# Talking-heads attention and a squared-ReLU FFN on one core: larger reserves in the planner, its order searched anew, and the reciprocals of the row sums on another engine

## The chip, the cores and the metric

The kernel runs on one core of a Trainium2 chip, as one launch. The time is device microseconds of one execution. Matrix products run on TensorE (PE), evictions from PSUM and elementwise work on ScalarE (ACT) and VectorE (DVE), small elementwise work and the loads' DMA issues on GpSimd (POOL), other DMA issues on SyncE (SP). Each engine works through its own list of instructions in order; semaphores tie the lists together.

## The reference

Eight batches, twelve heads, 448 positions, head dimension 64. The attention mixes the heads twice: the scores before the softmax with `w_pre`, the probabilities after it with `w_post`. An FFN with squared ReLU follows, 768 to 2048 to 768.

```python
scores = scale * np.matmul(q, k.transpose(0, 1, 3, 2))      # (8, 12, 448, 448)
scores = np.einsum('bhij,hg->bgij', scores, w_pre)
scores = scores - np.max(scores, axis=-1, keepdims=True)
attn = np.exp(scores)
attn = attn / (np.sum(attn, axis=-1, keepdims=True) + 1e-09)
attn = np.einsum('bhij,hg->bgij', attn, w_post)
attn_out = np.matmul(attn, v)
x = attn_out.transpose(0, 2, 1, 3).reshape(8 * 448, 768)
h = np.maximum(x @ w_in, 0.0)                               # (3584, 2048)
out = h * h @ w_out                                         # (3584, 768)
```

## The kernel before, in words

The kernel is written as some thousands of tasks. A task is a few instructions on one engine, with the tasks that it depends on, a planned cost and a priority. A planner (`_Plan`) plays the whole kernel through on the host when the program is built, and the program then has each engine's tasks in the planned order, with a semaphore wait wherever a dependency crosses engines. Nothing is decided at run time but how long each wait lasts; a wait stands only at the start of a task.

The stages for each batch, with the lines of their matmuls:

- **T** (L832, L836): q and k are transposed on PE into `qkt`.
- **QK** (L974, L981, L988): scores of one tile of 128 (or 64) query rows, evicted by DVE or ACT (L524, L523) into `stage`, one of two slots. In the first batch a direct form (**spr**, L915) gives part of the scores in the layout wanted.
- **Relayout** (`emit_rel`, L1033 and L1035): SP issues DMAs from `stage` to `dring`. They bring the twelve heads of ten query rows onto the partitions, a chunk of 120 rows. `dring` has 16 slots.
- **pre** (L1059, L1066, L1074): two chunks at a time are multiplied with the spread `w_pre`; ACT takes the exp (L1099) into `pring` (10 slots) and gives the row sums.
- **rec and fold** (L1122 and L1124, L1132): the reciprocal of the row sums is taken for a pair of chunks, `rinv`, and multiplied into a copy of the spread `w_post`, `wk2s`. For the first ten chunks both run on DVE, after that on POOL: there the reciprocal is a power of -1.
- **post** (L1164): `pring` times `wk2s` gives the mixed and normalized probabilities, transposed, evicted into `a2t`.
- **AV** (L1221, L1242) into `xt`; **F1** (L1293, L1301) with relu on ACT or DVE (L1338, L1339) and the square on DVE (L1348) into `h2t`; **F2** (L1432, L1440, L1380 for the last two tiles) into `osb`, one of two slots, and an output DMA issued by SP (L1478).

PE's units stand in ten queues (T, QK, pre, post, AV, spr, two of F1, two of F2). `ORDER` is a string with one character for each unit: which queue is next, and in which shape of the array it runs where a unit has more than one (rows, whole array, or quadrants). `next_unit` follows it, and TensorE never departs from it. All other engines take, among the tasks that are ready in the plan, the one that can start first; tasks marked FLEX (the evictions) go to ACT or DVE, wherever they are planned to end first. The string was found by a search that is not part of the kernel, against the planner's constants.

Those constants are estimates of the chip. `MODE_SWITCH` is charged where PE's shape changes. PE's instructions come in blocks of `BLOCK` = 256; `fetch` gives the planned time from the crossing of one block's end until the next block is there:

```python
return FETCH[0] + FETCH[1] * part["load"] + FETCH[2] * part["move"]
```

`part` is how much is moving in the two classes of DMAs, and `fetch_wait` puts the missing time before a unit. DMAs are of kind "load" (q, k, v, weights, and the outputs of the last two tiles) or "move" (the relayouts, and the other outputs). A DMA's data count as there at the end of its transfer plus `DMA_END` of its kind:

```python
t.end = max(t.end, now + DMA_END[t.dma[0]])
```

The DVE cost of a reciprocal is planned as 82 ns of the queue and 160 ns to the result, that on POOL as 700 and 750.

Of the kernel before, what the change touches and what calls it, by code (L numbers as in the profile page):

```python
# [7 lines left out]
ALU = mybir.AluOpType  # L8
DT = mybir.dt
# [4 lines left out]
DVE = "dve"  # L14
POOL = "pool"
# [4 lines left out]
MODE_SWITCH = 100.0  # L20
ACT_BIAS = 14.5
BLOCK = 256
FETCH = (2700.0, 2300.0, 1500.0)
EVENTS = {"tr": 0.12, "qk": 0.72, "di": 0.2, "sp": 0.3, "po": 0.61, "pr": 1.1, "av": 0.43, "o0": 0.43}
DMA_START = {"move": 2590.0, "load": 2640.0, "big": 1680.0}
DMA_AHEAD = 1600.0
DMA_END = {"move": 1450.0, "load": 1300.0}
INF = float("inf")
CODES = "0123456789abcdefghijklmnopqrst"
ORDER = (  # L30
    "00005bb05b0555555555555555555c12c555555513223555552c5001c353c00153355255233355555b332c22"
    "44443002h1g1b2q1h332g2236gh313c6722133hh31233gh6131hb2424443b32g26gh7q2b7371c63q1711r736"
    "2qh32002932t121j33933282b2s3c83338004224441200bgh11181c3s311s133s322rghg22b72b6h3163q633"
    "q32r42244413rbbh2ggb2002h716371623763q223837c738c33i3832bgh112rg0204244b20041328111ic31i"
    "3c3i33911tc11t22bj3c393c39342414431j313j2bqb2b62731762236733h3200q2162r21h13633g32r22728"
    "02000s131i113i14242b4334222931t333t111922813i3138422443411i332q2b6b2r2brb2gq0023733r3633"
    "qbrbq2rg2r200bh22913j12009111j3c381c383c3s313sc342442224193139111t333t2422444228318131i3"
    "13s32q2bqr227b3h2b2g733q333q20b6r120h2q0262000h7119331t111j33ct2228383138131ib4242224418"
    "3138331i24244413832q2bq2r2bh236331q33hgb21g72000r102h2173633633h24244420ttb2092b9238111i"
    "133i333i2t22btb2btbb2t238338331i42244431s31q2262713r1161733qh32qb2g2r2b273733r33gg12s22i"  # L40
    "22ss42244483i33s33i2qr262h2933933t33jq4q444hgqg6rgqhrh7ihgh6hgrhgg7hrqjjsjjit8isitijj"
)


# [72 lines left out]
class _Plan:  # L117
# [86 lines left out]
    def dma_next(self, go=False):  # L204
# [26 lines left out]
        if go:  # L231
# [5 lines left out]
            self.moving[t.dma[0]].pop(0)  # L237
            t.end = max(t.end, now + DMA_END[t.dma[0]])
            self._finish(t)
# [10 lines left out]
    def fetch(self, at):  # L250
        part = {}
        for q, xs in self.moving.items():
            part[q] = min(1.0, sum(x[1] for x in xs if x[0] <= at + 500.0) / 2500.0)
        return FETCH[0] + FETCH[1] * part["load"] + FETCH[2] * part["move"]

# [116 lines left out]
def bass_talking_heads_attention__then__ffn_squared_relu_kernel(  # L372
# [42 lines left out]
    with ExitStack() as es:  # L415
        def sb(name, shape, dtype):
            return es.enter_context(nc.sbuf_tensor(name, list(shape), dtype))
# [26 lines left out]
        rowsum = sb("rowsum", [128, B * NCP, 1], DT.float32)  # L444
# [2 lines left out]
        goods = sb("goods", [1, 128], DT.float32)  # L447
        flag = sb("flag", [1, 1], DT.int32)
        rinv = sb("rinv", [128, NPS, 1], DT.float32)
        minus1 = sb("minus1", [128, 2, 1], DT.float32)  # L450
        sb("align", [128, 64], DT.uint8)
        w_in_sb = sb("w_in_sb", [128, NFT, FF], DT.bfloat16)
        w_out_sb = sb("w_out_sb", [128, NFFT, F], DT.bfloat16)
# [38 lines left out]
        def program(guard):  # L492
# [9 lines left out]
            def add(name, engine, fn, deps, cost, prio, mode=None, group=None, instrs=0):  # L502
                return plan.add(name, engine, fn, deps, cost, prio, "ctr", 1, mode, group=group,
                                instrs=instrs)
# [28 lines left out]
            def fn_init(eng, en):  # L533
                eng.memset(mask[:, :, :], 1.0)
                eng.memset(wk1[:, :], 0.0)
                eng.memset(wrep[:, :], 0.0)
                eng.memset(wrepf[:, :], 0.0)
                eng.memset(maskf[:, :], 0.0)
                eng.memset(wkf[:, :, :], 0.0)
                eng.memset(wk2b[:, :, :], 0.0)  # L540
                eng.memset(rowsum[:, NCP - 1::NCP, :], 1.0)
                eng.memset(minus1[:, :, :], -1.0)
                return eng.memset(ident[:, :], 0.0)

            t_init = add("init", DVE, fn_init, [], {DVE: (950.0, 1050.0)}, -3e6)

            def fn_init2(eng, en):
# [127 lines left out]
            def members(g0):  # L675
                return (g0, g0 + 1) if g0 % NCP + 1 < NCH else (g0,)

            pairs = [b * NCP + c for b in range(B) for c in range(0, NCH, 2)]
            pre_of, exp_of, fold_of, post_of, a2_of = {}, {}, {}, {}, {}
# [366 lines left out]
            def old_users(g):  # L1046
                x = g - g % 2 - NPS
                return [d.get(y) for d in (post_of, fold_of) for y in (x, x + 1)]

            def emit_pre(g0):  # L1050
# [37 lines left out]
                for x, g in enumerate(gs):  # L1088
                    after_pre(g, t_pre, gr, x)

            def after_pre(g, t_pre, gr, x):
                b, c = divmod(g, NCP)
                pr = g % NPS

                def fn_exp(eng, en):
                    if guard:
                        return eng.activation(pring[:, pr, 0:S], ps[:, gr.banks[x], 0:S], AF.Exp,
                                              bias=nmax[:, pr, :], accum_out=rowsum[:, g, :])
                    return eng.activation(pring[:, pr, 0:S], ps[:, gr.banks[x], 0:S], AF.Exp,  # L1099
                                          accum_out=rowsum[:, g, :])  # L1100

                def fn_max(eng, en):
                    return eng.tensor_reduce(nmax[:, pr, :], ps[:, gr.banks[x], 0:S], AX.X, ALU.max,
                                             negate=True)

                t_max = None
                if guard:
                    t_max = add("max%d_%d" % (b, c), DVE, fn_max, [t_pre] + old_users(g),
                                {DVE: (540.0, 630.0)}, b * 1000.0 - 900 + c)
                t_exp = add("exp%d_%d" % (b, c), ACT, fn_exp, [t_pre, t_init, t_max] + old_users(g),  # L1110
                            {ACT: (517.0, 650.0)}, b * 1000.0 - 900 + c)
                exp_of[g] = t_exp
                gr.readers[x].append(t_exp)
                g0 = g - g % 2
                if g != members(g0)[-1]:
                    return
                n = g - g0 + 1
                p0 = g0 % NPS

                def fn_rec(eng, en):  # L1120
                    if en == POOL:
                        return eng.tensor_tensor(rinv[:, p0:p0 + n, :], rowsum[:, g0:g0 + n, :],  # L1122
                                                 minus1[:, 0:n, :], ALU.pow)
                    return eng.reciprocal(rinv[:, p0:p0 + n, :], rowsum[:, g0:g0 + n, :])  # L1124

                t_rec = add("rec%d_%d" % (b, c), DVE if g < 10 else POOL, fn_rec,
                            [exp_of[g0], t_exp] + old_users(g),
                            {DVE: (82.0, 160.0), POOL: (700.0, 750.0)}, b * 1000.0 - 900 + c)

                def fn_fold(eng, en):  # L1130
                    i0 = wk2b[:, :, :].rearrange("p a b -> p (a b)").unsqueeze(1)
                    return eng.tensor_tensor(  # L1132
                        wk2s[:, p0:p0 + n, :], i0.to_broadcast([128, n, PR]),
                        rinv[:, p0:p0 + n, :].to_broadcast([128, n, PR]), ALU.mult)

                t_fold = add("fold%d_%d" % (b, c), DVE if g < 10 else POOL, fn_fold,
                             [t_rec, t_wk2] + old_users(g),
                             {POOL: (330.0, 370.0), DVE: (200.0, 280.0)},
                             b * 1000.0 - 900 + c)
                t_fold.two = True  # L1140
                for y in members(g0):
                    fold_of[y] = t_fold
# [555 lines left out]
```

## Time and profile before

| | |
|---|---|
| three runs | 534.83, 539.58 and 539.79 us, median 539.58 us |
| the profiled execution | 537.8 us, span of its instructions 536.0 us |
| mean granted TensorE clock | 0.988 |
| busy: PE, ACT, DVE, POOL | 508.0, 412.3, 379.9, 290.8 us |
| POOL's reciprocals (L1122) | 179, 702 ns mean, 125.2 us |
| DVE's reciprocals (L1124) | 5, 155 ns mean |

The profile is one execution. Busy times are of the engine's own instructions. A row such as "PE ps L1074 <- DMA dring<-stage: 3.4, 4, 1.6" says that PE, before instructions of line 1074 that write `ps`, stood idle for 3.4 us in all, 4 times, at most 1.6 us, and that a DMA from `stage` to `dring` ended it. "issue" stands where no semaphore ended the wait. A wait for several things is put down to the one that came last by the profile. The rows of a timeline give start, duration, engine, line, operation, what it writes and reads, how many were merged, and in brackets the idle time before.

### The profile page before, as it was taken

How to read it: one execution, taken by the hardware profiler on the slowest of the kernel's cores; microseconds unless marked ns; L12 is line 12 of the kernel's file. 1: busy time of each engine (PE TensorE's matmuls, PEld its weight loads, DVE VectorE, ACT ScalarE, POOL GpSimd, SP SyncE). 2: the span in 40 equal slices, each digit the busy share in tenths (PEclk: the TensorE clock that was granted, in tenths of full speed). 3: DMA queues.
4: the chain of work that ended last, by engine and by line, in shares of the span. 5: the costliest groups of instructions: out<-in, count | busy, mean ns of one | idle time of the engine just before them, and what ended most of it. 6: DMA issues, size and time to landing. Idle time of an engine off the chain costs nothing.

```text
span 536.0 us, 24801 instructions
## 1 busy us (share of the span) xinstructions
PE 508.0 (95%) x10441; PEld 332.8 (62%) x10441; DVE 379.9 (71%) x806; ACT 412.3 (77%) x1181; POOL 290.8 (54%) x524
## 2 busy tenths in 40 slices
PE   8979999999999889989999899999989999989996
PEld 4435676667776546656566565666547766657963
DVE  7868977797987678765878768876857868536510
ACT  5979998888977878887787798888857888955421
POOL 9837788427954667446843587336844345522000
PEclk9989999999999999999999999999989999998999
DMA  9998999547964689457973689447963467532013
GB/s 172 192 184 145 196 183 193 112 87 146 178 154 75 137 183 173 93 127 135 180 166 67 140 150 224 92 91 163 193 134 64 105 141 142 113 72 61 3 29 93
DMA packets 81997, 70.87 MB, mean 132 GB/s; under 512 B 14038, under 2 KB 78422, under 8 KB 81878
## 3 DMA queue, kind: packets, MB, share of 16 engines
q1 hardware_dynamic: 48326, 46.40, 35.8%
q0 software_dynamic: 33392, 22.59, 31.0%
q8 instruction: 86, 1.41, 1.1%
q14 instruction: 33, 0.27, 0.1%
q10 hardware_dynamic: 160, 0.20, 0.1%
HBM read 45.63 MB, written 11.01 MB: 106 GB/s over the span
## 4 chain that ended last, share of the span: by engine, by line
PE 76%; DMA 7%; ACT 5%; DVE 4%; SPq 3%; issue 3%; POOL 0%; DVEq 0%; POOLq 0%
PE ps L1440 20%; PE ps L1301 17%; PE ps L1293 9%; PE ps L1164 6%; PE ps L1074 6%; DMA dring<-stage 5%; PE ps L1242 5%; SPq L1033 3%; ACT pring L1099 3%; PE ps L988 3%; PE ps L1380 2%; PE ps L1432 2%; PE ps L915 2%; DVE stage L524 2%; PE ps L836 2%
## 5 line engine op out<-in xcount | busy, mean ns | idle before, releaser
L1122 POOL TENSOR_TENSOR rinv<-rowsum,minus 128x2 f32<-128x2 f32 (+1 forms) x179 | 125.2, 702 | 185.9 <-ACT pring L1099 185.1
L1099 ACT ACTIVATE pring<-ps 128x448 bf16<-128x448 f32 x360 | 192.6, 563 | 23.0 <-PE ps L1074 13.2
L524 DVE CAST a2t<-ps 128x480 bf16<-128x480 f32 (+1 forms) x209 | 126.6, 641 | 37.6 <-PE ps L1164 36.7
L1440 PE MATMUL ps<-w_out_sb,h2t 64*128 64x384 bf16 (+1 forms) x1728 | 141.7, 324 | 0.2
L524 DVE CAST stage<-ps 128x448 bf16<-128x448 f32 x168 | 99.9, 618 | 31.1 <-PE ps L981 11.4
L1301 PE MATMUL ps<-xt,w_in_sb 64*64 64x448 bf16 (+4 forms) x1728 | 109.5, 329 | 0.1
L1440 PEld LDWEIGHTS ps<-w_out_sb,h2t 64*128 64x128 bf16 (+1 forms) x1728 | 75.3, 97 | 43.3 <-issue 2.0
L523 ACT ACTIVATE a2t<-ps 128x480 bf16<-128x480 f32 (+1 forms) x159 | 85.9, 580 | 20.8 <-PE ps L1164 20.0
L523 ACT ACTIVATE stage<-ps 128x448 bf16<-128x448 f32 x138 | 72.2, 556 | 18.7 <-PE ps L988 6.5
L1099 ACT ACTIVATION_READ_ACCUMULATOR pring<-ps 128x1 f32 x360 | 81.8, 227 | 0.0
L1301 PEld LDWEIGHTS ps<-xt,w_in_sb 64*64 64x64 bf16 (+1 forms) x1728 | 60.4, 103 | 29.8 <-issue 2.3
L1164 PEld LDWEIGHTS ps<-wk2s,pring 60*128 60x128 bf16 x2880 | 57.4, 94 | 28.0 <-issue 7.1
L1132 POOL TENSOR_TENSOR wk2s<-wk2b,rinv 128x120 bf16<-128x120 bf16 (+1 forms) x179 | 69.0, 388 | 10.2
L1164 PE MATMUL ps<-wk2s,pring 60*128 60x60 bf16 x2880 | 64.8, 187 | 4.4 <-issue 2.6
L1348 DVE TENSOR_TENSOR h2t<-h1t 128x448 bf16<-128x448 bf16 (+2 forms) x176 | 54.7, 336 | 11.2 <-ACT h1t L1338 10.1
L1074 PE MATMUL ps<-dring,wk 64*64 64x448 bf16 (+1 forms) x592 | 53.0, 360 | 10.0 <-DMA dring<-stage 3.4
L1293 PE MATMUL ps<-xt,w_in_sb 128*128 128x220 bf16 (+2 forms) x480 | 59.1, 276 | 0.0
L1338 ACT ACTIVATE h1t<-ps 128x448 bf16<-128x448 f32 (+2 forms) x88 | 39.1, 450 | 20.4 <-PE ps L1293 11.2
L1339 DVE TENSOR_SCALAR h1t<-ps 128x448 bf16<-128x448 f32 (+2 forms) x88 | 42.7, 492 | 16.5 <-PE ps L1301 13.1
L1293 PEld LDWEIGHTS ps<-xt,w_in_sb 128*128 128x128 bf16 x480 | 43.8, 98 | 12.3 <-issue 2.8
L523 ACT ACTIVATE osb<-ps 128x384 f32<-128x384 f32 x31 | 15.1, 492 | 27.2 <-PE ps L1432 8.6
L1242 PE MATMUL ps<-a2t,vraw 128*64 128x228 bf16 (+1 forms) x640 | 35.2, 261 | 0.0
(78 smaller groups left out, 464.5 us busy)
## 6 DMA issues: line engine op xcount, KB each, us to landing
dring<-stage SPq DMA_DIRECT2D x264, 105.0 KB
out_dram<-osb SPq DMA_DIRECT2D x45, 192.0 KB, 3.5
qraw<-in_q_dram POOLq DMA_DIRECT2D x42, 112.0 KB, 5.1
kraw<-in_k_dram POOLq DMA_DIRECT2D x42, 112.0 KB, 5.1
dring<-stage SPq DMA_DIRECT2D x70, 52.5 KB
w_in_sb<-in_moe_w_in_dram POOLq DMA_DIRECT2D x8, 384.0 KB, 10.0
w_out_sb<-in_moe_w_out_dram POOLq DMA_DIRECT2D x8, 384.0 KB, 8.8
vraw<-in_v_dram POOLq DMA_DIRECT2D x21, 128.0 KB
```

Source lines behind the costliest of these rows:

```text
L523: return eng.activation(o, i_, AF.Copy)
L524: return eng.tensor_copy(o, i_)
L1074: r_ = eng.matmul(ps[64 * y:64 * y + 64, gr.banks[x], 0:S], wk1[64 * x:64 * x + 64 - R0 * x, 64:128], dring[64 * x:64 * x + 64 - R0 * x, ( ...
L1099: return eng.activation(pring[:, pr, 0:S], ps[:, gr.banks[x], 0:S], AF.Exp, accum_out=rowsum[:, g, :])
L1122: return eng.tensor_tensor(rinv[:, p0:p0 + n, :], rowsum[:, g0:g0 + n, :], minus1[:, 0:n, :], ALU.pow)
L1132: return eng.tensor_tensor(wk2s[:, p0:p0 + n, :], i0.to_broadcast([128, n, PR]), rinv[:, p0:p0 + n, :].to_broadcast([128, n, PR]), ALU.mult)
L1164: r_ = eng.matmul(ps[:, gr.banks[x], o0:o0 + PR], pring[64 * x:64 * x + PR, pr + y, j0:j0 + 2 * PJ], wk2s[64 * x:64 * x + PR, pr + y, :], ...
L1242: r_ = eng.matmul(ps[kk * 64:kk * 64 + 64, g.banks[x_], x * n:(x + 1) * n], vraw[:, h, s, :], a2t[half][:, s, h, a0:a0 + n], start=(rest a ...
L1293: r_ = eng.matmul(ps[:, g.banks[ph], 0:n], w_in_sb[:, ft, t * 128:(t + 1) * 128], xt[:, ft, c0:c1], start=(ft == 0), stop=(ft == NFT - 1))
L1301: r_ = eng.matmul(ps[z:z + w, g.banks[x], 0:n], w_in_sb[64 * y:64 * y + 64, ft, t * 128 + z:t * 128 + z + w], xt[64 * y:64 * y + 64, ft, c ...
L1348: return eng.tensor_tensor(h2t[:, t16, o0:o0 + n], h1t[:, s, 0:n], h1t[:, s, 0:n], ALU.mult)
L1440: r_ = eng.matmul(ps[z:z + w, g.banks[hh], 0:FH], h2t[64 * y:64 * y + 64, t16, col + z:col + z + w], w_out_sb[64 * y:64 * y + 64, t16, hh ...
```

## The change

Three things: two of the planner's constants, the order string, and the engine of the reciprocals.

```diff
-FETCH = (2700.0, 2300.0, 1500.0)
+FETCH = (3500.0, 2300.0, 1500.0)
...
-DMA_END = {"move": 1450.0, "load": 1300.0}
+DMA_END = {"move": 2000.0, "load": 1300.0}
...
 ORDER = (
-    "00005bb05b0555555555555555555c12c555555513223555552c5001c353c00153355255233355555b332c22"
...
-    "22ss42244483i33s33i2qr262h2933933t33jq4q444hgqg6rgqhrh7ihgh6hgrhgg7hrqjjsjjit8isitijj"
+    "0000b15555011505555555555555552c5555555051325530cc51555cc3c233003555c352315553155533ccc2"
...
+    "s228i244438333i22283s3393t322t933rqr46444h7hghgghqghggghgiirqh7hgh8hr6gsjg8ttj88j98jj"
 )
...
-        minus1 = sb("minus1", [128, 2, 1], DT.float32)
...
-                eng.memset(minus1[:, :, :], -1.0)
...
                 def fn_rec(eng, en):
-                    if en == POOL:
-                        return eng.tensor_tensor(rinv[:, p0:p0 + n, :], rowsum[:, g0:g0 + n, :],
-                                                 minus1[:, 0:n, :], ALU.pow)
                     return eng.reciprocal(rinv[:, p0:p0 + n, :], rowsum[:, g0:g0 + n, :])
 
-                t_rec = add("rec%d_%d" % (b, c), DVE if g < 10 else POOL, fn_rec,
-                            [exp_of[g0], t_exp] + old_users(g),
-                            {DVE: (82.0, 160.0), POOL: (700.0, 750.0)}, b * 1000.0 - 900 + c)
+                t_rec = add("rec%d_%d" % (b, c), DVE, fn_rec, [exp_of[g0], t_exp] + old_users(g),
+                            {DVE: (82.0, 160.0)}, b * 1000.0 - 900 + c)
```

The whole string of 965 characters is replaced. The fold keeps its engine. Since the other engines' orders and the choice of ACT or DVE for each eviction come out of the same plan, they change with it.

More of the change, by code (lines that the diff above doesn't have):

```diff
@@ L30 @@
 ORDER = (
-    "00005bb05b0555555555555555555c12c555555513223555552c5001c353c00153355255233355555b332c22"
[L32 to L40, printed above, removed]
-    "22ss42244483i33s33i2qr262h2933933t33jq4q444hgqg6rgqhrh7ihgh6hgrhgg7hrqjjsjjit8isitijj"
+    "0000b15555011505555555555555552c5555555051325530cc51555cc3c233003555c352315553155533ccc2"
+    "44443c020hg11qr1g13333ch62217gc31h2g332h313g33hg2b1h424b244c33hgg11ghq1c173r3711r26gc663"
+    "73r2392002j122j33j3128321s322833i200424432411002ghb118133i3ci313s31g722bbghq22b6rhbg33r3"
+    "63g2422444b2rb7002bh1gh6363c1g67b2r673h3c38212i33832833hg42b24732440b20q02081118131i31c8"
+    "3c39332t2b2t113t3b29122931j33c3j242444313qbbbq237131h2263q733r0202qb62br200h2263g33rb272"
+    "b8b00238111s133832424443339222j31t331t11822bi13i3c3s242444133qb2b6rbbbh22g630202733h6333"
+    "g2r12r2q12gr2b0720931t3020t1119c1381c383318113s342442b22439223j33t131j3424422248338131s3"
+    "13811r2bq226r2273h33612g633q32bhbq20206b2rh002002r39111t113t333t22288331s331i14242224438"
+    "111i3c3i24244421i336133g3br2b72qb2gb1gh33rq22r001r200637336372t41244bjb20j20292b438133i1"
+    "12i333s13t2b2j2b292bj23833i131s4b24443s13q2bbg2rb2h2613633733h2q2262r2br36333g3r2bh42s21"
+    "s228i244438333i22283s3393t322t933rqr46444h7hghgghqghggghgiirqh7hgh8hr6gsjg8ttj88j98jj"
 )
```

## The prediction

> **What bounds the kernel now.** I read the page first, then who TensorE waits for, then narrow windows around its longest waits, then its order of instructions there.
>
> ```profile
> span 536.0 us, 24801 instructions
> PE 508.0 (95%) x10441; PEld 332.8 (62%) x10441; DVE 379.9 (71%) x806; ACT 412.3 (77%) x1181; POOL 290.8 (54%) x524
> ...
> q8 instruction: 86, 1.41, 1.1%
> ```
>
> TensorE (PE) is busy 95% of the span; VectorE (DVE), ScalarE (ACT) and GpSimd (POOL) stand idle 156, 124 and 245 us. So a gain can only come from PE's idle time, or from work taken off PE, and the change takes no matmul's columns away. The instruction queue q8 brings 86 pieces, one for each 536 / 86 = 6.2 us; PE issues some 21,000 instructions by my count over the units, 82 of the planner's blocks of 256, so I take q8 to be PE's. Whom PE waits for (us in total, times, longest):
>
> ```profile
> PE ps L1074 <- DMA dring<-stage: 3.4, 4, 1.6
> PE ps L1074 <- DVE osb L524: 3.1, 2, 2.2
> PE ps L974 <- issue: 2.8, 2, 2.6
> PE ps L1164 <- issue: 2.6, 2, 1.8
> ...
> PE ps L836 <- issue: 1.4, 1, 1.4
> PE ps L1074 <- DVE h2t L1348: 1.4, 1, 1.4
> PE ps L1164 <- DVE stage L524: 1.4, 2, 1.0
> ...
> PE ps L988 <- ACT osb L523: 1.1, 1, 1.1
> PE ps L1074 <- DVE stage L524: 0.9, 2, 0.7
> ...
> PE ps L1066 <- DVE stage L524: 0.4, 1, 0.4
> PE ps L1074 <- issue: 0.4, 1, 0.4
> PE ps L915 <- issue: 0.3, 1, 0.3
> PE ps L981 <- issue: 0.3, 1, 0.3
> ...
> PE ps L1164 <- DVE wk2s L1132: 0.2, 1, 0.2
> ```
>
> Three kinds matter. "issue" sums to 2.8 + 2.6 + 1.4 + 0.4 + 0.3 + 0.3 = 7.8 us: waits for no semaphore. Relayouts (stage to dring) are 3.4 us. The third hides behind the name osb, and I come to it below. First, what an "issue" wait is:
>
> ```profile
> 391.88 1.33 PE L1301 MATMUL ps<-xt,w_in_sb 64*64 64x448 bf16 x24
> 393.02 0.38 PE L1074 MATMUL ps<-dring,wk 64*64 64x448 bf16 x4
> 393.21 0.38 PE L974 MATMUL ps<-qkt 64*64 64x448 bf16 x3
> 396.24 0.37 PE L974 MATMUL ps<-qkt 64*64 64x448 bf16 x1 [2.65 <-issue]
> ```
>
> The unit at L974 is four matmuls written by one function with no wait inside, and PE stops after the third. Only missing instructions explain that; I take all of "issue" to be fetches. The next view (window, its length, PE busy, granted clock, DMA share, GB/s) shows that a long wait is paid twice:
>
> ```profile
> 28.00:33.00 5.00, 4.33 (x125) 1.00 1.24 206
> 35.30:38.70 3.40, 3.40 (x28) 0.50 0.84 160
> 299.10:304.10 5.00, 5.00 (x94) 1.00 0.61 122
> 393.60:396.20 2.60, 0.00 (x0) 1.00 0.88 159
> 397.10:400.50 3.40, 3.40 (x34) 0.50 0.58 130
> 479.00:481.10 2.10, 0.02 (x4) 1.00 0.42 94
> 482.40:485.80 3.40, 3.40 (x42) 0.50 0.42 111
> ```
>
> After the waits of 1.8 us (at 34, L1164), 2.65 us (at 396) and 2.2 us (at 481) the clock stands at 0.50 for 3.4 us, and 1.7 us of work is lost each time; after those of 1.4 us (at 28, L836) and 1.6 us (at 299, L1074) it stays at 1.00. The Trainium skill ("TensorE: Matmul & The Clock Gate", Part 1) says that the clock halves after at least one idle window of about 3.4 us. No wait here is that long, so the trace disagrees with that length, and it decides; by the rule no dip would hang on these waits, and the forecast below would be 533.1 us. What stops PE at 481:
>
> ```profile
> 476.65 5.61 SPq L1478 DMA_DIRECT2D out_dram<-osb  x4
> ...
> 480.56 0.49 ACT L523 ACTIVATE osb<-ps 128x384 f32<-128x384 f32 x1 [3.44 <-DMA out_dram<-osb]
> 480.56 0.56 DVE L524 COPY osb<-ps 128x384 f32<-128x384 f32 x1 [3.25 <-DMA out_dram<-osb]
> ...
> 481.18 0.38 PE L1074 MATMUL ps<-dring,wk 64*64 64x448 bf16 x4 [2.16 <-DVE osb L524]
> ```
>
> Both evicting engines stand at the head of their queues for an osb slot that an output DMA has not left; PE then lacks a bank. So the 2.2 us at L1074 (of the 3.1) and, by the same name, the 1.1 us at L988 are late outputs. The output DMAs are planned as kind "move", like the relayouts, so DMA_END["move"] speaks for both: 3.4 + 2.2 + 1.1 = 6.7 us.
>
> **The change, part by part.** The sum is made against the profiled execution's own 537.8 us (span 536.0). The three runs shown are 534.83 to 539.79 with a median of 539.58, 1.8 above it. A measurement of this kernel tells about 1% from no change: 534.2 and 545.0 against that median.
>
> *The reserve on fetches.* FETCH[0] goes from 2700 to 3500 ns: 0.8 us more are planned for each fetch, and the new order has to space short matmuls for it. If that shortens each wait by up to 0.8: 2.6 to 1.8, 0.2 to 0, 1.8 to 1.0, 0.8 to 0, 1.4 to 0.6, and 0.4 + 0.3 + 0.3 to 0 make 0.8 + 0.2 + 0.8 + 0.8 + 0.8 + 1.0 = 4.4 us. Of its two clock dips the one after 1.8 us goes (1.0 is shorter than waits that had none), and the one after 2.65 may stay: 1.7. Together 6.1. Bounds: nothing, and all, 7.8 + 3.4 = 11.2. I take 6.1, as the rows' lengths against the reserve say.
>
> The Trainium skill speaks against this part: "Runtime: NRT & Kernel Launch", Instruction fetch mechanics, says that crossing a 16 KiB block is one tail-bump that is mostly hidden. The 2.65 us inside a unit disagrees; by the rule this term would be 0.
>
> *The reserve on relayouts and outputs.* DMA_END["move"] grows by 0.55 us. The dring waits are 1.6 (299), about 1.3 and 0.5 in the two others: 0.55 + 0.55 + 0.5 = 1.6. Both osb waits shrink by 0.55: 1.1. The dip at 482 follows a wait of 2.2; at 1.6 it would be like the one at 299, without a dip: 1.7. Together 4.4. Bounds: 0, and 6.7 + 1.7 = 8.4.
>
> *The new order.* Its characters each name a queue and a shape. Read out unit by unit (965 in both, the same in every queue), with the shapes that the unit functions give, the old one changes TensorE's shape (whole array, row, column, quadrants, 32 columns) 225 times and the new one 240 times; instructions differ by under 0.1%, so there are as many fetches. The price of one change:
>
> ```profile
> 299.05 0.38 PE L1074 MATMUL ps<-dring,wk 64*64 64x448 bf16 x4 [1.58 <-DMA dring<-stage]
> 299.37 0.94 PE L1242 MATMUL ps<-a2t,vraw 128*64 128x220 bf16 x16
> ```
>
> From L1074 to another shape it is 0.32 us (299.05 to 299.37), to the same shape 0.19 (393.02 to 393.21): 0.13, say 0.12. Fifteen more are +1.8 us, on PE and covered by nothing; the bounds are that and nothing, where a change falls into a wait. Work by shape is otherwise equal. Waits for loads at the start are not costed: both orders need the same loads first.
>
> *Reciprocals to DVE.*
>
> ```profile
> L1122 POOL TENSOR_TENSOR rinv<-rowsum,minus 128x2 f32<-128x2 f32 (+1 forms) x179 | 125.2, 702 | 185.9 <-ACT pring L1099 185.1
> ...
> L1124 DVE RECIPROCAL rinv<-rowsum 128x2 f32<-128x2 f32 x5 | 0.7, 155 | 0.5 <-ACT pring L1099 0.4
> ```
>
> ```profile
> 21.18 0.21 DVE L1124 RECIPROCAL rinv<-rowsum 128x2 f32<-128x2 f32 x2
> 21.31 0.64 DVE L524 CAST a2t<-ps 128x480 bf16<-128x480 f32 x1
> ```
>
> POOL loses 125.2 us, 0.70 for each of 179. The chain from exp to the folded weights gets 0.55 shorter, but PE waits for the fold 0.2 us in all, so that is worth at most 0.2: nothing. What hides POOL's work now is the distance that the order keeps between exp and post. DVE gains 179 instructions. Two of them hold its queue from 21.18 to 21.31, 0.065 each although one lasts 0.155: 11.6 us low, 27.7 high. I take 11.6, since these are the same operation on the same tile; DVE goes to 391.5 us, 73% of the span, and some evictions may go to ACT. Cover is DVE's 156 us of idle time. PE's waits that DVE ends (h2t 1.4, stage 1.4 + 0.9 + 0.4, the other 0.9 of osb) are 5.0 us; at 3% more load +0.15.
>
> It also adds a wait. The reciprocal needs both of its exp's on ACT; what queues behind it on DVE are evictions (stage, a2t, relu) and squares, for whose banks and tiles PE waits. The five on DVE waited 0.4 us, 0.08 each, so 179 would wait 14.3 us. DVE's idle time reaches PE at 5.0 of 156, 3%: 0.5. The bounds are nothing, and all 14.3. I take 0.5, and 0.6 for this part.
>
> **Sum:** 537.8 - 6.1 - 4.4 + 1.8 + 0.6 = 529.7, rounded to 530 us.
>
> **The rivals.**
> 1. *The reserves take all of it.* -11.2 - 8.4 + 1.8 + 0.6: 520.6 us. For it: the new order need not be dense where the old one was. Against: a wait of 2.65 us is over three times the reserve, and DMA times vary between executions.
> 2. *The waits move (the change does not do what it says).* The new order has its own dense stretches and late slots, as many as before: 537.8 + 1.8 + 0.6 = 540.2. For it: 86 fetches make only some ten visible waits, so a few unlucky stretches decide, and the order has changed everywhere. Against: these places are what the larger constants price. In the same family lies that only the fetch term is nothing, because pieces arrive as late as before for the new stretches: 537.8 - 4.4 + 1.8 + 0.6 = 535.8. The rule of the Trainium skill quoted above gives this time too.
> 3. *Slower: DVE's head.* Reciprocals wait there for ACT, evictions queue up, and PE runs out of banks, as it did at 481 for another reason. All 14.3 us reach PE, and such waits keep the clock dips (the 3.4 us not saved): 537.8 - 7.1 + 1.8 + 14.3 + 0.15 = 547.0. For it, a like case in the steady state:
>
> ```profile
> DVE h2t L1348 <- ACT h1t L1338: 10.1, 23, 1.5
> ```
>
> Squares wait 10.1 us for ACT. Against: of that and all else at DVE's head only 5.0 reach PE now. It decides from 10.5 - 1.8 = 8.7 us on, 49 ns per reciprocal; over 1% slower needs 79 ns.
>
> **How the numbers follow.** The forecast gets 0.46 with its own range 524 to 534; rival 1 0.12; rival 2 0.18 and the fetch term alone 0.06; rival 3 0.18. Faster by over 1% hold the forecast and rival 1, with the forecast's slow edge going to "same": 0.58. Rival 2 with the fetch term makes most of "same", 0.24; rival 3 0.18. The range reaches from rival 1 to near rival 3, 521 to 546; about 0.1 lies above and 0.07 below.
>
> **What would show it.** In the new profile PE's "issue" waits should come to about 3.4 us and no unit should break off for over 2 us; PE's waits for dring and for osb together to about 4; windows at clock 0.50 inside the kernel to one instead of three; PE's busy time should hardly move. The page should list some 184 DVE reciprocals, none on POOL, POOL near 166 us and DVE near 391. The forecast is wrong if "issue" stays near 8 us or the dips stay at three (rival 2), or if DVE's wait for ACT before its reciprocals nears 14 us and PE's waits for DVE grow by as much (rival 3).

## The result and the profile after

| | before | after |
|---|---|---|
| median, us | 539.03 (534.83 to 539.79, 4 runs) | 558.78 (556.13 to 561.82, 4 runs) |
| the profiled execution, us | 537.8, span 536.0 | 561.8, span 560.0 |

The kernel became slower: ratio 1.0397, 95% interval 1.0347 to 1.0448. The forecast was 530 us, faster. Medians are of all runs, while the ratios here and below leave out the runs more than 1.5% above the fastest of their kernel, so a ratio need not be the quotient of the medians. The page of the kernel after, in the rows that stood for before:

```profile
span 560.0 us, 24784 instructions
...
PE 517.4 (92%) x10442; PEld 333.3 (60%) x10442; DVE 390.8 (70%) x966; ACT 419.1 (75%) x1199; POOL 168.0 (30%) x345
...
L1119 DVE RECIPROCAL rinv<-rowsum 128x2 f32<-128x2 f32 (+1 forms) x184 | 28.9, 158 | 29.3 <-ACT pring L1097 28.5
```

The span grew by 24.0 us: PE's busy time by 517.4 - 508.0 = 9.4 and its idle time by (560.0 - 517.4) - (536.0 - 508.0) = 14.6. The reciprocals did as announced: 184 on DVE, POOL at 168, DVE at 390.8. Whom PE waits for in the kernel after (total, times, longest):

```profile
PE ps L1072 <- DMA dring<-stage: 8.2, 5, 2.1
PE ps L1158 <- DVE stage L523: 4.2, 1, 4.2
PE ps L1158 <- issue: 3.3, 1, 3.3
PE ps L1236 <- DVE osb L523: 2.9, 1, 2.9
PE ps L1158 <- DVE osb L523: 2.8, 1, 2.8
PE ps L1434 <- DVE osb L523: 2.4, 1, 2.4
PE ps L1295 <- issue: 2.0, 1, 2.0
...
PE ps L1158 <- ACT osb L522: 1.5, 1, 1.5
...
PE ps L1287 <- issue: 1.3, 1, 1.3
PE ps L1072 <- issue: 0.9, 1, 0.9
...
PE ps L834 <- issue: 0.5, 1, 0.5
...
PE ps L913 <- issue: 0.3, 1, 0.3
```

"issue" sums to 8.3 us (7.8 before), the relayouts to 8.2 (3.4), osb with 0.4 at L1287 to 10.0 (4.2). Many of the long waits come with stretches at half clock, here in windows of the kernel after (length, PE busy, granted clock, DMA share, GB/s; seven rows and their sum, three rows shown):

```profile
35.50:42.30 6.80, 4.66 (x58) 0.50 0.39 80
...
134.50:141.30 6.80, 5.53 (x44) 0.50 0.60 123
...
380.20:383.70 3.50, 3.50 (x26) 0.51 0.57 109
sum 30.80, PE 26.73; mean PE 3.82
```

Seven stretches instead of three: half of 26.73, 13.4 us of work, against 5.1. That is 8.3 of the 9.4 us by which PE's busy time grew. So nearly the whole loss is waits and what they do to the clock. Where the longest wait arises, in a timeline of the kernel after:

```profile
307.92 7.04 SPq L1031 DMA_DIRECT2D dring<-stage  x8
...
315.06 1.18 SPq L1472 DMA_DIRECT2D out_dram<-osb  x2
316.34 2.63 SPq L1033 DMA_DIRECT2D dring<-stage  x3
316.98 0.98 ACT L522 ACTIVATE stage<-ps 128x448 bf16<-128x448 f32 x2 [4.51 <-DMA dring<-stage]
316.98 1.16 DVE L523 CAST stage<-ps 128x448 bf16<-128x448 f32 x2 [4.33 <-DMA dring<-stage]
...
317.67 0.40 PE L1158 MATMUL ps<-wk2s,pring 60*128 60x60 bf16 x16 [4.18 <-DVE stage L523]
```

SP issues relayouts without a pause, 0.88 us each. Both evicting engines stand for over 4 us at the head of their queues until a `stage` slot has been read; then PE has no PSUM bank to write. In the kernel before both engines together waited 8.2 us for such slots, here 18.3; first the rows of before, then of after:

```profile
DVE stage L524 <- DMA dring<-stage: 4.2, 5, 1.6
ACT stage L523 <- DMA dring<-stage: 4.0, 5, 1.8
```

```profile
DVE stage L523 <- DMA dring<-stage: 11.5, 4, 4.3
...
ACT stage L522 <- DMA dring<-stage: 6.8, 4, 4.5
```

The question was why the relayouts are late, though the change adds no byte to them.

### The profile page after: what moved, and what is told of

Same layout as the page of the kernel before. It is cut to its first block, busy times and chain, and to the rows that moved or that the text cites. A ratio compares the mean times of both kernels' runs of the same rounds, so it can differ in the third digit from the quotient of the medians.

```text
span 560.0 us, 24784 instructions
## 1 busy us (share of the span) xinstructions
PE 517.4 (92%) x10442; PEld 333.3 (60%) x10442; DVE 390.8 (70%) x966; ACT 419.1 (75%) x1199; POOL 168.0 (30%) x345
## 3 DMA queue, kind: packets, MB, share of 16 engines
q1 hardware_dynamic: 48326, 46.40, 36.8%
## 4 chain that ended last, share of the span: by engine, by line
PE 72%; SPq 10%; DMA 9%; issue 3%; POOL 2%; ACT 2%; DVE 2%; DVEq 0%; POOLq 0%
PE ps L1295 18%; PE ps L1434 17%; SPq L1031 9%; PE ps L1287 8%; PE ps L1158 6%; PE ps L1072 5%; PE ps L1236 5%; DMA dring<-stage 4%; DMA out_dram<-osb 3%; PE ps L986 2%; PE ps L1374 2%; PE ps L1426 2%; PE ps L834 2%; DMA qraw<-in_q_dram 2%; PE ps L913 1%
## 5 line engine op out<-in xcount | busy, mean ns | idle before, releaser
L1434 PE MATMUL ps<-w_out_sb,h2t 64*128 64x384 bf16 (+1 forms) x1728 | 144.1, 327 | 2.4 <-DVE osb L523 2.4
L523 DVE CAST stage<-ps 128x448 bf16<-128x448 f32 x174 | 103.4, 617 | 32.4 <-DMA dring<-stage 11.5
L1295 PE MATMUL ps<-xt,w_in_sb 64*64 64x448 bf16 (+4 forms) x1728 | 111.7, 329 | 2.2 <-issue 2.0
L522 ACT ACTIVATE stage<-ps 128x448 bf16<-128x448 f32 x132 | 69.3, 555 | 22.4 <-PE ps L986 9.5
L1097 ACT ACTIVATION_READ_ACCUMULATOR pring<-ps 128x1 f32 x360 | 79.3, 220 | 0.0
L1332 ACT ACTIVATE h1t<-ps 128x448 bf16<-128x448 f32 (+2 forms) x103 | 45.7, 449 | 29.0 <-PE ps L1287 11.6
L1072 PE MATMUL ps<-dring,wk 64*64 64x448 bf16 (+1 forms) x596 | 54.2, 363 | 9.8 <-DMA dring<-stage 8.2
L1287 PE MATMUL ps<-xt,w_in_sb 128*128 128x220 bf16 (+2 forms) x468 | 58.6, 278 | 1.7 <-issue 1.3
L1287 PEld LDWEIGHTS ps<-xt,w_in_sb 128*128 128x128 bf16 x468 | 43.5, 100 | 13.8 <-issue 2.5
L1119 DVE RECIPROCAL rinv<-rowsum 128x2 f32<-128x2 f32 (+1 forms) x184 | 28.9, 158 | 29.3 <-ACT pring L1097 28.5
L1333 DVE TENSOR_SCALAR h1t<-ps 128x448 bf16<-128x448 f32 (+2 forms) x73 | 36.3, 503 | 10.3 <-PE ps L1287 4.6
L1236 PE MATMUL ps<-a2t,vraw 128*64 128x228 bf16 (+1 forms) x640 | 36.7, 267 | 2.9 <-DVE osb L523 2.9
```

Of the source, the lines that this page charges most:

```text
L522: return eng.activation(o, i_, AF.Copy)
L523: return eng.tensor_copy(o, i_)
L1072: r_ = eng.matmul(ps[64 * y:64 * y + 64, gr.banks[x], 0:S], wk1[64 * x:64 * x + 64 - R0 * x, 64:128], dring[64 * x:64 * x + 64 - R0 * x, ( ...
L1236: r_ = eng.matmul(ps[kk * 64:kk * 64 + 64, g.banks[x_], x * n:(x + 1) * n], vraw[:, h, s, :], a2t[half][:, s, h, a0:a0 + n], start=(rest a ...
L1287: r_ = eng.matmul(ps[:, g.banks[ph], 0:n], w_in_sb[:, ft, t * 128:(t + 1) * 128], xt[:, ft, c0:c1], start=(ft == 0), stop=(ft == NFT - 1))
L1295: r_ = eng.matmul(ps[z:z + w, g.banks[x], 0:n], w_in_sb[64 * y:64 * y + 64, ft, t * 128 + z:t * 128 + z + w], xt[64 * y:64 * y + 64, ft, c ...
```

## The experiments

Ratios are against the kernel before, run on the same chip in the same session (its medians in the five sessions: 536.1, 537.2, 536.2, 537.6, 538.9 us), with 95% intervals. The expectation of each kernel stands as it was written before its run.

**Which part? Four kernels that mix the parts.** In old_constants the kernel before gets the two new constants and keeps its order:

```diff
-FETCH = (2700.0, 2300.0, 1500.0)
+FETCH = (3500.0, 2300.0, 1500.0)
-DMA_END = {"move": 1450.0, "load": 1300.0}
+DMA_END = {"move": 2000.0, "load": 1300.0}
```

> The kernel before with the two new constants alone: PE's order is the old one, the other engines' orders are planned anew with the larger reserves. Theory DVE: no change, 536 to 543 us. Theory ORDER: the same, 533 to 545 us. Theory FIT: 545 to 555 us.

Measured 536.26 us, 1.0033 (0.9994 to 1.0073): nothing measurable. In old_recdve the kernel before gets the reciprocals on DVE, with everything that the change deletes for it:

```diff
-        minus1 = sb("minus1", [128, 2, 1], DT.float32)
...
-                t_rec = add("rec%d_%d" % (b, c), DVE if g < 10 else POOL, fn_rec,
+                t_rec = add("rec%d_%d" % (b, c), DVE, fn_rec, [exp_of[g0], t_exp] + old_users(g),
```

> The kernel before (old order, old constants), with the reciprocals alone moved to DVE. Theory DVE (reciprocals at the head of DVE's queue wait for ACT, evictions queue behind, PE runs out of banks): most of the 20 us come with this edit, 552 to 560 us, and DVE's waits for ACT before its reciprocals near 28 us. Theory ORDER (the new order leaves the DMAs that SP issues late; the engine of the reciprocals does not matter): 533 to 545 us. Theory FIT (an order fits only the constants and engines it was searched with, and any edit of the plan costs): 545 to 555 us.

Measured 552.12 us, 1.0229 (1.0123 to 1.0336). Next, new_recpool is the kernel after with these lines put back:

```diff
+        minus1 = sb("minus1", [128, 2, 1], DT.float32)
...
+                t_rec = add("rec%d_%d" % (b, c), DVE if g < 10 else POOL, fn_rec,
```

> The changed kernel (new order, new constants), with the reciprocals back on GpSimd as a power of -1. Theory DVE: the time comes back, 536 to 545 us. Theory ORDER: 553 to 564 us, with PE's waits for late relayouts and outputs as in the changed kernel. Theory FIT: slower than the changed kernel, 560 to 575 us.

Measured 548.77 us, 1.0224 (1.0121 to 1.0328). And old_order_rest_new is the kernel after with the old order:

```diff
 ORDER = (
-    "0000b15555011505555555555555552c5555555051325530cc51555cc3c233003555c352315553155533ccc2"
+    "00005bb05b0555555555555555555c12c555555513223555552c5001c353c00153355255233355555b332c22"
```

> The changed kernel with the old order string: new constants and reciprocals on DVE. Theory DVE: 552 to 560 us. Theory ORDER: 535 to 547 us. Theory FIT: 550 to 565 us, since this order was searched for neither.

Measured 556.42 us, 1.0401 (1.0309 to 1.0493). So the order isn't the main loss, and the edit for the reciprocals seemed to be. I took that to mean the work or the wait on DVE.

**Is it DVE's queue?** dummy_waits keeps POOL's reciprocals and adds unread ones on DVE, with the wait for the exps; in dummy_no_wait these read a constant and wait for nothing:

```diff
+                def fn_dum(eng, en):
+                    return eng.reciprocal(rdum[:, g0 % 64:g0 % 64 + n, :], rowsum[:, g0:g0 + n, :])
```

Expected of dummy_waits:

> The kernel before (old order, old constants, reciprocals on GpSimd), with a second reciprocal of the same row sums on DVE at the place where the moved one would stand; it waits for the same exp's and nobody reads its result. Theory HEAD (an instruction at DVE's head that waits for ACT lets evictions, then relayouts, then PE run late): 546 to 556 us, DVE's waits for ACT there 15 to 28 us. Theory WORK (179 more instructions on DVE, or any other plan of the engines): 546 to 556 us. Theory POOL (an emptier GpSimd issues its loads earlier and they hold up the relayouts): 534 to 541 us.

Of dummy_no_wait:

> As the one before, but the second reciprocal reads a constant tile and waits for nothing; its place in DVE's list is about where the exp starts. Theory HEAD: 535 to 542 us. Theory WORK: 546 to 556 us. Theory POOL: 534 to 541 us.

They took 538.68 us, 1.0023 (0.9975 to 1.0071), and 537.78 us, 1.0017 (0.9969 to 1.0064). In dummy_waits most of the wait is there (24.4 us in old_recdve), from its list of waits:

```profile
DVE rdum L1133 <- ACT pring L1101: 22.8, 32, 1.4
```

179 more instructions on DVE and 22.8 us of waiting at its head cost nothing measurable. recdve_reserve comes at it from the other side: old_recdve with 1.5 us planned between the exps and their reciprocal, so that it is issued when they are done:

```diff
-            s.avail = max(s.avail, t.end + SEM_LAT)
+            s.avail = max(s.avail, t.end + SEM_LAT + (1500.0 if s.name[:3] == "rec" else 0.0))
```

> The kernel before with the reciprocals on DVE (the 552 us kernel), where the planner counts the exp's of a reciprocal as there 1.5 us later, so that DVE has evictions ahead of it and does not wait at its head. Theory HEAD: most of the 16 us come back, 536 to 544 us, and DVE's waits for ACT before reciprocals fall from 24 us to under 5. Theory WORK: 546 to 556 us. Theory POOL: 546 to 556 us.

DVE's wait for the exps falls to 3.4 us, and the time is 556.95 us, 1.0372 (1.0271 to 1.0473). This run alone would not decide, because the later reciprocals have a price of their own: PE now waits 6.3 us for the folded weights (`wk2s`). With dummy_waits, the theory of DVE's head falls. recdve_pool_busy is old_recdve with the old power of -1 left on POOL, its result unread (and `minus1` with it):

```diff
+                    return eng.tensor_tensor(rdum[:, g0 % 64:g0 % 64 + n, :], rowsum[:, g0:g0 + n, :],
+                                             minus1[:, 0:n, :], ALU.pow)
```

> The kernel before with the reciprocals on DVE (the 552 us kernel); GpSimd still takes the power of the row sums as before, into a tile that nobody reads, so its load and its issues stay as they were. Theory HEAD: 546 to 556 us. Theory WORK: 546 to 556 us. Theory POOL: 534 to 541 us.

537.48 us, 1.0022 (0.9984 to 1.0059): the loss is gone. I read this as POOL's work holding something back that does harm when it comes early, and that was a wrong turn.

**What does a busy POOL hold back?** All four still look for the cause in POOL. ghost plans the unread instruction on POOL and issues neither it nor its waits; tiny_power issues a short copy in its place; gated_loads (from old_recdve) holds POOL's loads back with waits for pre; new_pool_busy is the kernel after with the unread power.

```diff
+                    plan.add("rdu%d_%d" % (b, c), POOL, lambda eng, en: None, [exp_of[g0], t_exp],
...
+                    return eng.tensor_copy(rdum[:, g0 % 64:g0 % 64 + n, :], rowsum[:, g0:g0 + n, :])
...
+                    ts.append(load_v(b, u, h0, rows, [last_av.get(b - 1)] + after, after,
```

Expected of ghost:

> The 537 us kernel with reciprocals on DVE and the unread power on GpSimd, planned to the same order on every engine, but the program leaves the power and its wait out: GpSimd is as empty as in the 552 us kernel, its list has the order of the 537 us kernel. Theory LIST (what costs is the order of the lists that a plan without the power gives: loads ahead of folds, evictions elsewhere): 535 to 541 us. Theory EMPTY (GpSimd's own time and waits are what holds its loads back on the chip): 547 to 556 us, and SP's relayout issues as slow as in the 552 us kernel.

Of tiny_power:

> The same 537 us kernel, with the unread power replaced by an unread copy of the row sums, planned as long as the power: GpSimd waits for the same exp's at the same places, but works much less. Theory LIST: 535 to 541 us. Theory EMPTY: between the two, 540 to 550 us if the power's duration counts, 535 to 541 if its wait does.

Of gated_loads:

> The 552 us kernel (reciprocals on DVE, GpSimd emptier), where the loads of q, k and v of later batches wait on the chip for the pre step that the planner has them follow, so they can't run ahead. Theory LOADS (loads run ahead of PE, share the DMA engines with the relayouts, and slow them): 535 to 545 us. If loads running ahead are not the way: 547 to 558 us.

Of new_pool_busy:

> The changed kernel (new order, new constants, reciprocals on DVE), with the unread power on GpSimd as before. If GpSimd's lost work is the cause there as in the old order: 535 to 545 us. If the new order has a cost of its own: 546 to 556 us.

ghost 537.12 us, 1.0012 (0.9965 to 1.006); tiny_power 537.44, 1.0042 (1.0001 to 1.0084); gated_loads 553.08, 1.0335 (1.025 to 1.0421); new_pool_busy 544.19, 1.0133 (1.0054 to 1.0212). ghost has POOL as empty as old_recdve (168.1 us busy in both) and is fast, gated_loads holds the loads back and is slow: neither POOL's work nor the loads matter. What the fast ones share is a line that seemed to be housekeeping. Of the kernels with the old order, all that keep `minus1` (`rdum` adds 256 bytes) are fast, all without it slow.

**Is it an address?** `minus1` has 8 bytes per partition in a slot of 32. Without it every later tile starts 32 bytes lower: `stage` at 108,896, which is 96 past a multiple of 256, instead of 108,928, 128 past one. In new_pad the kernel after gets an unused tile in its place; before_shift, stage_shift and dring_shift are the kernel before, plan and order untouched, with 224 unused bytes ahead of `align`, of `stage` alone, or of `dring` alone (32 more behind the last two keep the rest). The lines are those of new_pad and of stage_shift:

```diff
+        sb("pad0", [128, 32], DT.uint8)
...
+        sb("pad0", [128, 224], DT.uint8)
         stage = sb("stage", [IT, 2, H, S], DT.bfloat16)
+        sb("pad1", [128, 32], DT.uint8)
```

Expected of new_pad:

> The changed kernel with one unused tile of 32 bytes a partition, where the removed tile minus1 (8 bytes, in a slot of 32) stood; nothing else differs, the plan least of all. Theory ADDRESS (without minus1 every later tile, stage and dring among them, lies 32 bytes lower, and the relayouts' packets take longer): 540 to 548 us, with SP's relayout issues at a median of 853 ns instead of 928. Theory LIST (the order of the engines' lists): 556 to 562 us.

Of before_shift:

> The kernel before with an unused tile of 224 bytes ahead of the large tiles, so that each lies at the same place modulo 256 bytes as in the changed kernel (stage, dring and osb at 96 instead of 128). Theory ADDRESS: 547 to 556 us, SP's relayout issues at a median of 900 ns or more. Theory LIST: 534 to 540 us.

Of stage_shift:

> The kernel before with stage alone at 96 modulo 256 bytes; all other tiles as before. Stage is the source of the relayouts. If the place of the source counts: 547 to 556 us; if that of the destination: 534 to 540 us; if both by halves: 540 to 547 us. The Trainium skill (DMA: Bandwidth & Descriptors, How a descriptor splits into AXI transactions) has reads start at multiples of 256 bytes in beats of 32: a row of 896 bytes needs 30 beats on average at 128 and 33 at 96, so it speaks for the source.

Of dring_shift:

> The kernel before with dring alone at 96 modulo 256 bytes; all other tiles as before. Dring is the destination of the relayouts. If the place of the source counts: 534 to 540 us; if that of the destination: 547 to 556 us; if both by halves: 540 to 547 us.

new_pad 544.87 us, 1.0114 (1.0058 to 1.0171); before_shift 554.89, 1.0304 (1.0239 to 1.0369); stage_shift 554.82, 1.0333 (1.026 to 1.0405); dring_shift 537.78, 0.9979 (0.9938 to 1.002). The kernel before loses 17 us when nothing but the place of `stage` changes, and nothing when `dring`, where the same DMAs write, is moved by as much. Each page's row of the queue q1 (all but a few of SP's DMAs: packets, MB, share of 16 engines), with spans; first before, then stage_shift, dring_shift and the kernel after:

```profile
span 536.0 us, 24801 instructions
...
q1 hardware_dynamic: 48326, 46.40, 35.8%
q0 software_dynamic: 33392, 22.59, 31.0%
```

```profile
span 551.2 us, 24801 instructions
...
q1 hardware_dynamic: 48326, 46.40, 37.6%
```

```profile
span 536.1 us, 24801 instructions
...
q1 hardware_dynamic: 48326, 46.40, 36.2%
```

```profile
q1 hardware_dynamic: 48326, 46.40, 36.8%
q0 software_dynamic: 33392, 22.59, 29.8%
```

Share times span is what a DMA engine spends on the same packets: 191.9 us before, 207.3 in stage_shift, 194.1 in dring_shift, 206.1 after. With `stage` 32 bytes off, 14 to 15 us more; the loads of q0 stay (166.2 and 166.9 us). SP pays in its issues (the relayouts of one DMA each; ns, shortest, median, longest; the 112 issues of relayouts of two keep a median of 769), before and in stage_shift:

```profile
L1035 SPq DMA_DIRECT2D dring<-stage x301: 672/853/2256, 30.6 to 460.3; - x151
```

```profile
L1037 SPq DMA_DIRECT2D dring<-stage x301: 682/923/2291, 31.4 to 477.2; - x151
```

And the evicting engines wait for the slots, in stage_shift and in dring_shift:

```profile
DVE stage L526 <- DMA dring<-stage: 15.5, 10, 2.8
ACT stage L525 <- DMA dring<-stage: 12.3, 8, 2.9
```

```profile
DVE stage L526 <- DMA dring<-stage: 7.1, 6, 2.2
ACT stage L525 <- DMA dring<-stage: 5.3, 4, 2.4
```

27.8 us against 12.4 (8.2 before). PE's own waits for dring and for `stage` evictions come to 12.7 us in stage_shift, 8.9 in dring_shift and 6.1 before. In new_pad, where the kernel after has its addresses back, the evicting engines wait 8.4 us for the slots instead of 18.3.

**What about the address, and what is left?** stage_64 moves `stage` alone, to 192 past a multiple of 256; newrec_oldconst_pad is new_pad with the old constants (of which one is shown).

```diff
+        sb("pad0", [128, 64], DT.uint8)
         stage = sb("stage", [IT, 2, H, S], DT.bfloat16)
+        sb("pad1", [128, 192], DT.uint8)
...
-FETCH = (3500.0, 2300.0, 1500.0)
+FETCH = (2700.0, 2300.0, 1500.0)
```

Expected of stage_64:

> The kernel before with its plan and order unchanged and two unused tiles of 64 and 192 bytes per partition, one ahead of stage and one behind it, so that stage alone starts 64 bytes later, at 192 bytes past a multiple of 256; dring and osb keep their place in the 256. It tells what about stage's address counts. If only the 64-byte line counts (the starts at 128 are on one, those at 96 are not), 192 is as good as 128: packets of 896 bytes at 60 to 61 ns, SP's issue of a relayout at about 0.85 us, the time 536 to 539 us. If what counts is in how many pieces of 32 bytes, with reads beginning at multiples of 256, a row has to be read (the rule in the Trainium skill, DMA: Bandwidth & Descriptors, How a descriptor splits into AXI transactions), a row from 192 takes 32 of them, from 128 it takes 30 and from 96 it takes 33: packets at some 64 ns, two thirds of the way from 60 to 66, and the time two thirds of the way from 537.6 to 554.8, some 549 us.

Of newrec_oldconst_pad:

> The kernel after (new order, reciprocals on DVE) with the old constants (2700 and 1450) and an unused tile of 32 bytes in place of the removed one, so that stage, dring and osb lie where they lay before. The new order with the new constants at the old addresses gave 544.9 us, 7 us above the kernel before. If those 7 us belong to the order string, which only fits one set of stalls and shape changes, they stay: 541 to 548 us. If they belong to the new constants, with which the planner sorts the other engines' tasks, they go: 535 to 540 us. The constants alone, in the kernel before, gave 536.3 us, which speaks for the order. A time above 548 would say that order and constants belong together, the order having been searched for them.

stage_64 took 549.15 us, 1.0275 (1.0171 to 1.038), and its page has:

```profile
span 545.3 us, 24801 instructions
...
q1 hardware_dynamic: 48326, 46.40, 37.1%
```

37.1% of 545.3 is 202.3 us: 10.4 above before, where stage_shift has 15.4 above, so 0.68 of it. One trace does not fix the second digit: the twelve kernels with `stage` at 128 have 191.6 to 194.1 us, which makes it 0.62 to 0.68. The share in time, 0.0275 of 0.0333, is too uncertain to tell. SP's issues of one DMA each are slower here too (median 914 ns). The theory of a 64-byte line falls (it wanted 536 to 539 us). The Trainium skill ("DMA: Bandwidth & Descriptors", How a descriptor splits into AXI transactions) says that reads begin at multiples of 256 bytes and go in pieces of 32. By that rule the twelve rows of 896 bytes, which lie end to end so that their starts alternate by 128, take 30 pieces each on average from 128, 32 from 192 and 33 from 96, so two thirds of the excess: the runs agree, 0.62 to 0.68. The 39,168 packets of 896 bytes on q1, taken alone from the traces, agree more closely. They last 60.4 ns in the mean before, 64.7 in stage_64 and 66.6 in stage_shift, ratios of 1.07 and 1.10, as 32 / 30 and 33 / 30 (60.1 to 61.7 in all kernels at 128, 66.2 to 67.7 in all at 96).

newrec_oldconst_pad took 546.18 us, 1.0176 (1.0084 to 1.0267), and new_recpool, with POOL's reciprocals and the old address, 1.0224: neither the constants nor the reciprocals are what is left, so the order is, by elimination. The new order with both at once as they were before has not been run. All 18 runs and the kernel after, by `stage`'s place past a multiple of 256:

| order | `stage` | ratios |
|---|---|---|
| old | 128 | 0.998 (dring_shift), 1.001 (ghost), 1.002 (dummy_waits, dummy_no_wait, recdve_pool_busy), 1.003 (old_constants), 1.004 (tiny_power) |
| old | 192 | 1.028 (stage_64) |
| old | 96 | 1.023 (old_recdve), 1.030 (before_shift), 1.033 (stage_shift), 1.034 (gated_loads), 1.037 (recdve_reserve), 1.040 (old_order_rest_new) |
| new | 128 | 1.011 (new_pad), 1.013 (new_pool_busy), 1.018 (newrec_oldconst_pad), 1.022 (new_recpool) |
| new | 96 | 1.040 (the kernel after) |

At 96 the two orders with the new constants and DVE's reciprocals come out alike (old_order_rest_new and the kernel after, 1.040 each), so the costs of order and address do not simply add. What the order costs is read from new_pad, whom PE waits for there, and its timeline at 257 us:

```profile
PE ps L1159 <- issue: 3.3, 1, 3.3
PE ps L1159 <- DVE osb L524: 2.5, 1, 2.5
PE ps L1237 <- DVE osb L524: 2.3, 1, 2.3
PE ps L1159 <- DVE stage L524: 2.2, 1, 2.2
...
PE ps L1435 <- DVE osb L524: 1.6, 1, 1.6
...
PE ps L1073 <- DMA dring<-stage: 1.2, 1, 1.2
PE ps L1288 <- issue: 1.1, 1, 1.1
...
PE ps L835 <- issue: 0.9, 1, 0.9
PE ps L1159 <- ACT osb L523: 0.9, 1, 0.9
```

```profile
250.81 4.69 SPq L1473 DMA_DIRECT2D out_dram<-osb  x4
255.61 2.51 SPq L1034 DMA_DIRECT2D dring<-stage  x3
256.72 0.49 ACT L523 ACTIVATE osb<-ps 128x384 f32<-128x384 f32 x1 [2.70 <-DMA out_dram<-osb]
...
257.33 0.38 PE L1237 MATMUL ps<-a2t,vraw 128*64 128x228 bf16 x2 [2.31 <-DVE osb L524]
```

osb sums to 7.3 us against 4.2 before. Four outputs stand behind one another on SP, and the evictions start at 256.72, when the second of them has landed (256.69 in the trace). new_pad has such waits of the evicting engines near 257, 362 and 489 us (and one of 1.1 us near 197), and so, 5 to 8 us later, do newrec_oldconst_pad and new_recpool, and 14 to 21 us later the slower kernel after; new_pool_busy has only the last two. In the profile before there is a single one of over 1 us, at 481. Late outputs are the largest growth but not the whole of what is left. The profiled span of new_pad is 4.9 us longer than that of before: PE's busy time grew by 2.5, its idle time by 2.4. In the idle time osb grew by 3.1 and waits for the exps (`pring`) by 1.7, while the relayouts fell by 2.2 and "issue" by 1.6. No experiment singles out any of these. No kernel that ran beats the kernel before.

## Why the prediction was wrong, by its steps

*The deletion of `minus1`* is the step that failed most, by being absent. The diff shows it, and the sum gave it neither a term nor a word, as if a tile of 8 bytes could only be worth its memset. It moves the source of the relayouts by 32 bytes: 17 us in the kernel before (stage_shift), 558.8 - 544.9 = some 14 us of the kernel after, of its 20 (15 by the ratios, 1.0397 and 1.0114). Of the 29.1 us between the sum of 529.7 and the measured 558.8, that is 13.9. Another 10.5 are the two reserves, which bring no net gain in new_pad, and 544.9 - 540.2 = 4.7 are what its new order loses beyond that. No row of the profile before shows an address, but the relayouts' weight was there to be read: SP's issues, the 3.4 us, q1's 35.8%.

*The reserve on fetches*, -6.1: came to nothing. Without the address effect, in new_pad, "issue" still sums to 6.2 us (the rows above and 0.6 + 0.3), with one wait of 3.3, and the stretches at half clock inside the kernel are four, not one. old_constants shows that with the old order the constant itself buys nothing measurable. That "issue" is fetches was only argued, and the traces bear it out: each of the seven waits before and the six after ends 1.2 to 1.6 us after a piece of q8 has come in, and these come one in 6.2 us. The term also took a wait's length to decide whether a dip follows; it does not (see the last section). The mis-step was to let every visible wait shrink by the reserve; a new order makes new places. The fetches are not hidden (8.3 us after), against the rule of the Trainium skill that the prediction quoted ("Runtime: NRT & Kernel Launch", Instruction fetch mechanics), though its result for this term, nothing, was nearer.

*The reserve on relayouts and outputs*, -4.4: half right where the address is restored. In new_pad PE waits 1.2 us for dring (I expected 1.8), but 7.3 for osb (before 4.2, expected 3.1): the new order has at least three places with late outputs and not one. The sum, 8.5, is above the 7.6 of before.

*The new order*, +1.8: not measured by itself. A count over the matmuls in the traces, by whether they have more than 64 rows and whether they have up to 32, up to 64 or more columns, gives 233 changes of shape before and 250 after, 17 more where 15 were forecast; no run shows their price.

*Reciprocals to DVE*, +0.6: not contradicted. The wait was under-estimated, 28.5 us instead of 14.3, and still costs nothing that shows: dummy_waits and ghost are 0.2 and 0.1% above before, with intervals that end at 0.7 and 0.6%. That nothing PE needs is queued behind DVE's head at most of these times would explain it; that is argued, not shown. Rival 3 was the only one on the slower side, and in the old order its mechanism is shown to be wrong; that the time was beyond its 547 had another cause.

Rival 2, the waits move, is what the rest of the change did: 540.2 forecast, 544.9 measured with the address put back.

## What to carry to other kernels

Removing or adding a small tile moves every later one: before crediting a change to its engines or its order, put the addresses back with an unused tile and time that. Where DMAs read rows from SBUF and the engines wait for them, the start of the source within 256 bytes is a tuning parameter; here 32 bytes were worth 3%, and 96, 128 and 192 are the only starts that were tried. A control that adds back work also adds back what came with it (here the tile): ghost and its kin were needed to see that the work didn't matter.

## What the hardware showed that I had not expected

- The same 48,326 packets of q1 cost a DMA engine 191.9, 202.3 and 207.3 us with the relayouts' source 128, 192 and 96 bytes past a multiple of 256; with the destination moved instead, to 96, they cost 194.1 us and the time stayed at 0.998.
- Half-clock stretches can double: 6.8 us at 35.5 and at 134.5 in the kernel after, both with further idle time of PE inside (4.66 and 5.53 us busy); the others last 3.4, also the one at 271 with 0.5 us idle inside.
- The length of one wait does not decide whether a stretch at half clock follows. In the kernel after, waits of 2.0 us (ending at 425.2) and 2.8 us (at 510.9) have none. The starts of all seven stretches there (35.53, 66.25, 134.52, 192.54, 271.05, 318.84, 380.28) lie whole multiples of 3.413 us apart, and so do the three in the kernel before (35.27, 397.09, 482.42). It fits these traces that PE's idle time between two such marks decides: the 2.8 us are split by a mark into about 1.9 and 0.9, while in new_pad two waits of 1.0 and 1.2 us, with 2.0 us of idle time ahead of one mark, are followed by a stretch (127.7). No experiment varied this.
- 179 more instructions on DVE, 32 of which wait, 22.8 us in all, at the head of an engine that is then 73% busy, cost nothing that could be measured (1.0023, 0.9975 to 1.0071).
